# Recurrence feeding an FFN on one core: r transposed raw, exponentials multiplied out of PSUM, row loads of four batches, masks and small products dealt out anew

## The chip, the cores and the metric

One core of a Trainium2 chip. The metric is the time of one execution in microseconds (us). The two kernels compute the same thing in bf16 with fp32 sums, and both are correct. A run is called fast unless it is over 1.5% above the fastest of its kernel; only fast runs are compared.

## The reference, cut

```python
# r, k, v, w: (4 batches, 8 heads, 768 steps, 48);  u: (8, 48)
for t in range(S):                                    # the recurrence (RWKV-6)
    y[t]  = r[t] @ (state + (u * k[t]) outer v[t])
    state = w[t] * state + k[t] outer v[t]
x = y as (3072 tokens, 384)                           # the FFN
out = ((x @ w1) * (x @ w2)) @ w3 @ w_out              # d_ff = 1024
```

The kernel takes the steps in 6 chunks of 128. With cumulative sums c of log w in a chunk, it forms K = k·exp(−c) and R = r·exp(c up to the step before), a masked 128x128 product M of K and R per head, then y = M·v + R·state + dv. Here dv is the diagonal term v·(sum of r·k·u). w3 and w_out are multiplied together once, beforehand.

## The kernel before

The work is cut into 13 units (one or two batches of one chunk) and 8 FFN blocks (up to 512 tokens). A list scheduler in the kernel plans one order of issue from model durations and tuned priority tables; each engine then executes its own operations strictly in that order. The parts that matter, cut:

```python
UNITS = [(0, 0, 1), (0, 1, 1), (0, 2, 2)] + [(c, b, 2) for c in range(1, 6) for b in (0, 2)]
DMA_KR = PE_DIAG = set(range(9, 13))      # K, R and r*k of these units are transposed by DMA
SP_LOADS = {("w", 0)}                     # every other row load is issued by GpSimd (k, r, v change type)
NI = 5                                    # row buffers of two batches: win, kin, rin; six for v
# --- unit t (cut) ---
ACT  lw = Ln(w)
PE   CS = LT^T @ lw                       # running sums in PSUM, by step
ACT  iw = Exp(-lw);  NEt = Exp(-CS);  Et = Exp(CS)          # all to SBUF
DVE  rw = r * iw
DVE  KR[k] = k * NEt;  KR[r] = rw * Et                      # both inputs in SBUF
DVE  rk = r * k;  ruk = rk * u;  dg = reduce_sum(ruk)
POOL dv = v * dg
PE   transposes of KR (k and r) -> PSUM;  ACT KRT = copy    # or two DMA transposes
PE   M = K^T R;  DVE Mbf = M * mask                         # 5 of 24 masks: ACT copy, then POOL select
PE   y = R state + M v;  DVE yb = y + dv;  PE transpose;  ACT xT = copy
PE   kv;  DVE T = kv + S;  POOL Sbf = T * pc, S = T * pc
# --- block n: 8 pairs of a, b matmuls; ACT a copy; DVE abT = a * b; then out = abT @ (w3 w_out) ---
```

## Time and profile before

| kernel before | value |
|---|---|
| median of the first 3 runs | 186.49 us (184.28 to 186.94) |
| profiled run: time, span, mean granted clock | 186.09 us, 184.4 us, 0.986 |
| busy: TensorE, VectorE, ScalarE, GpSimd | 157.5, 131.4, 110.1, 108.0 us |

The busy shares, the stretches and the chain of waits are shown in the prediction. These are 2 us stretches of the kernel before. The columns are the stretch, busy time (with instruction count) of TensorE, its weight loads, VectorE, ScalarE and GpSimd, then the granted clock, the DMA share and GB/s.

```profile
92.00:94.00 2.00, 1.01 (x7) 0.39 (x4) 2.00 (x3) 0.48 (x1) 1.98 (x3) 1.00 2.14 159
94.00:96.00 2.00, 0.00 (x0) 0.00 (x0) 2.00 (x3) 0.00 (x0) 1.83 (x2) 1.00 2.37 162
96.00:98.00 2.00, 1.72 (x27) 1.51 (x28) 1.99 (x4) 0.80 (x1) 0.00 (x0) 0.87 1.24 112
98.00:100.00 2.00, 2.00 (x21) 2.00 (x20) 1.81 (x3) 1.36 (x1) 0.00 (x0) 0.50 0.96 176
100.00:102.00 2.00, 2.00 (x73) 1.67 (x73) 0.58 (x1) 1.72 (x2) 0.04 (x1) 0.78 1.08 370
```

TensorE stands still for 3.27 us, and 1.2 us after it starts again its clock is halved. The Trainium skill says in "TensorE: Matmul & The Clock Gate", section HAM oscillation — how this bites in real kernels, that idle gaps of more than about 3.4 us bring the half-rate clock back. This trace roughly agrees, at 3.27 us.

### The profile page before, as it was taken

How to read it: one execution, taken by the hardware profiler on the slowest of the kernel's cores; microseconds unless marked ns; L12 is line 12 of the kernel's file. 1: busy time of each engine (PE TensorE's matmuls, PEld its weight loads, DVE VectorE, ACT ScalarE, POOL GpSimd, SP SyncE). 2: the span in 40 equal slices, each digit the busy share in tenths (PEclk: the TensorE clock that was granted, in tenths of full speed). 3: DMA queues.
4: the chain of work that ended last, by engine and by line, in shares of the span. 5: the costliest groups of instructions: out<-in, count | busy, mean ns of one | idle time of the engine just before them, and what ended most of it. 6: DMA issues, size and time to landing. Idle time of an engine off the chain costs nothing.

```text
span 184.4 us, 4285 instructions
## 1 busy us (share of the span) xinstructions
PE 157.5 (85%) x1753; PEld 98.8 (54%) x1753; DVE 131.4 (71%) x205; ACT 110.1 (60%) x184; POOL 108.0 (59%) x108
## 2 busy tenths in 40 slices
PE   1242698999989998799929999999999999999991
PEld 0131486787767765346519545665546446545560
DVE  6258858497599986899996996876897286445420
ACT  4261475989988698776817728789732435351321
POOL 7999969976987999989970895132402202000000
PEclk9999999999999999999996999999999999999998
DMA  4999999999999999999999950496604501100332
GB/s 52 193 158 205 195 188 237 155 207 199 165 164 168 187 183 192 176 153 156 142 145 223 112 77 4 88 183 133 117 0 100 146 0 37 52 0 0 128 128 87
DMA packets 95971, 24.13 MB, mean 131 GB/s; under 512 B 88192, under 2 KB 93824, under 8 KB 95952
## 3 DMA queue, kind: packets, MB, share of 16 engines
q0 software_dynamic: 79408, 16.06, 105.1%
q1 hardware_dynamic: 16544, 7.80, 18.4%
q8 instruction: 13, 0.21, 0.5%
q14 instruction: 6, 0.05, 0.1%
HBM read 27.79 MB, written 4.72 MB: 176 GB/s over the span
## 4 chain that ended last, share of the span: by engine, by line
PE 73%; DVE 10%; POOL 5%; issue 4%; DMA 3%; ACT 3%; DVEq 0%; POOLq 0%
PE banks L802 18%; PE banks L807 16%; PE banks L825 14%; PE banks L567 4%; PE banks L676 4%; PE banks L694 3%; DMA kin<-in_k_dram 3%; PE banks L733 3%; PE banks L598 2%; PE banks L753 2%; DVE Mbf L700 2%; PE banks L555 2%; DVE yb L742 2%; DVE KR L630 2%; PE banks L727 2%
## 5 line engine op out<-in xcount | busy, mean ns | idle before, releaser
L814 ACT COPY a_sb<-banks 128x512 f32<-128x512 f32 (+2 forms) x64 | 30.1, 483 | 30.1 <-PE banks L802 23.4
L818 DVE TENSOR_TENSOR abT<-a_sb,banks 128x512 bf16<-128x512 f32 (+2 forms) x64 | 34.1, 550 | 17.4 <-PE banks L807 14.1
L802 PE MATMUL banks<-xT,w_bf 128*128 128x512 bf16 (+2 forms) x192 | 39.3, 335 | 1.4 <-DVE abT L818 1.4
L807 PE MATMUL banks<-xT,w_bf 128*128 128x512 bf16 (+2 forms) x192 | 39.3, 329 | 0.0
L825 PE MATMUL banks<-w,abT 128*128 128x384 bf16 x192 | 33.7, 326 | 0.0
L802 PEld LDWEIGHTS <-w_bf 128*128 128x128 bf16 x192 | 17.4, 102 | 14.9 <-issue 1.9
L825 PEld LDWEIGHTS <-abT 128*128 128x128 bf16 x192 | 18.1, 98 | 11.7
L700 DVE TENSOR_TENSOR Mbf<-banks,mask 128x1024 bf16<-128x1024 f32 x19 | 23.0, 1218 | 1.0 <-PE banks L694 1.0
L807 PEld LDWEIGHTS <-w_bf 128*128 128x128 bf16 x192 | 16.7, 99 | 13.0
L658 POOL TENSOR_TENSOR dv<-vin,dg 128x768 bf16<-128x768 bf16 (+1 forms) x13 | 18.9, 1463 | 7.8 <-issue 2.4
L682 ACT COPY KRT<-banks 128x2048 bf16<-128x2048 bf16 (+1 forms) x9 | 15.1, 1674 | 7.8 <-PE banks L676 7.4
L513 POOL DMA_DIRECT2D vin<-in_v_dram x13 | 14.8, 1140 | 7.8 <-issue 7.8
L676 PE MATMUL banks<-I,KR 128*128 128x128 bf16 x128 | 11.4, 250 | 8.7 <-DVE KR L628 7.4
L780 POOL TENSOR_TENSOR Sbf<-Tst,pc 128x384 bf16<-128x384 f32 (+1 forms) x11 | 9.2, 835 | 13.6 <-PE banks L727 13.5
L742 DVE TENSOR_TENSOR yb<-banks,dv 128x768 bf16<-128x768 f32 (+1 forms) x13 | 11.6, 894 | 5.5 <-PE banks L733 5.2
L513 POOL DMA_DIRECT2D kin<-in_k_dram x13 | 14.4, 1112 | 1.4 <-DVE rk L634 0.6
L833 ACT COPY osb<-banks 128x384 f32<-128x384 f32 x16 | 7.7, 481 | 12.6 <-PE banks L825 12.5
L591 ACT ACTIVATE lw<-win 128x768 bf16<-128x768 f32 (+1 forms) x13 | 10.5, 806 | 7.8 <-DMA win<-in_w_dram 7.8
L676 PEld LDWEIGHTS <-KR 128*128 128x128 bf16 x128 | 9.4, 113 | 9.8 <-DVE KR L628 7.6
L513 POOL DMA_DIRECT2D rin<-in_r_dram x13 | 14.6, 1127 | 0.0
L758 ACT COPY xT<-banks 128x768 bf16<-128x768 bf16 (+1 forms) x13 | 9.8, 755 | 7.8 <-PE banks L753 7.8
L706 POOL TENSOR_SCALAR_AFFINE_SELECT Mbf<-Mbf 128x1024 bf16<-128x1024 bf16 x5 | 6.2, 1231 | 13.9 <-ACT Mbf L703 13.9
(66 smaller groups left out, 249.8 us busy)
## 6 DMA issues: line engine op xcount, KB each, us to landing
out_dram<-osb SPq DMA_DIRECT2D x24, 192.0 KB, 2.0
win<-in_w_dram POOLq DMA_DIRECT2D x11, 384.0 KB, 10.2
kin<-in_k_dram POOLq DMA_DIRECT2D x11, 192.0 KB, 10.4
rin<-in_r_dram POOLq DMA_DIRECT2D x11, 192.0 KB, 9.8
vin<-in_v_dram POOLq DMA_DIRECT2D x11, 192.0 KB, 9.7
w_bf<-in_moe_w_dram POOLq DMA_DIRECT2D x4, 512.0 KB, 10.4
w_bf<-in_moe_w_dram POOLq DMA_DIRECT2D x4, 384.0 KB, 6.3
wo_bf<-in_moe_w_out_dram POOLq DMA_DIRECT2D x1, 768.0 KB, 9.6
```

Of the source, the lines that this page charges most:

```text
L513: op(eng, 60 if eng == "SP" else 700 + 250 * nb, lambda: e.dma_start(dst[:, :nb * H], ap), w=[key], prio=turn_of(f"{src}in_{t}"), dma=nb * ...
L591: op("ACT", act(N), lambda: nc.scalar.activation(LW[:, :, :D], ww, Act.Ln), r=[kw, "table"], w=[f"lw{s}"], prio=pr, name=f"ln_{t}")
L658: op("POOL", pool(N), lambda: nc.gpsimd.tensor_mul(dvs, vv, dgs[:, :, None].to_broadcast([C, bh, D])), r=[f"dg{s}", kv], w=[f"dv{s}"], pri ...
L676: nc.tensor.transpose(o[:, b, q, :], KRs[:, x, h:h + 2, :].rearrange("t h d -> t (h d)"), I128)
L682: nc.scalar.copy(KRTs.rearrange("p x b q t -> p x (b q t)"), o[:, :, :nb * HP * C])
L700: nc.vector.tensor_mul(Mbf[m].rearrange("s j q t -> s (j q t)"), o.rearrange("s j f -> s (j f)"), mask.rearrange("s q t -> s (q t)"))
L742: nc.vector.tensor_add(ybs.rearrange("t b (q e d) -> t e (b q) d", e=2, d=D), o, dvs.rearrange("t (b q e) d -> t e (b q) d", b=nb, e=2))
L802: nc.tensor.matmul(banks[:, g.at(A), :T], lhsT=wt[:, di, fi * P:(fi + 1) * P], rhs=xT[x][:, di, :T], start=(di == 0), stop=(di == DI - 1))
L807: nc.tensor.matmul(banks[:, g.at(Bk), :T], lhsT=wt[:, di, fi * P:(fi + 1) * P], rhs=xT[x][:, di, :T], start=(di == 0), stop=(di == DI - 1))
L814: nc.scalar.copy(a_sb[sa][:, :T], banks[:, g.at(A), :T])
L818: nc.vector.tensor_mul(abT[x][:, fi, :T], a_sb[sa][:, :T], banks[:, g.at(Bk), :T])
L825: nc.tensor.matmul(banks[:, g.at(O), :DM], lhsT=abT[x][:, fi, tt * P:(tt + 1) * P], rhs=w34[:, fi, :], start=(fi == 0), stop=(fi == FI - 1))
```

## The change

Its intent is to take work off the two elementwise engines, at the price of more TensorE work, and to issue fewer and larger row loads:

- r is transposed as loaded. The sums are made a second time, transposed (CT), so exp(CT) multiplies r^T straight out of PSUM. iw, rw and one multiply go.
- exp(−sum) is written back into PSUM, and k is multiplied there.
- From chunk 1 on, one load brings four batches. Buffers hold three chunks.
- Masks, r·k, r·k·u, dv, copies and state products are dealt out anew among VectorE, ScalarE and GpSimd: 13 masks instead of 5 go over ScalarE and GpSimd, and 13 of the r·k and r·k·u products go to GpSimd.
- Only units 11 and 12 keep DMA transposes, which wait for the last row. The first three blocks get their own buffers.
- The tuned tables, and with them the whole order of issue, are new.

```diff
-DMA_KR = set(range(9, 13))
-PE_DIAG = set(range(9, 13))
+DMA_KR = set(range(11, 13))
+DMA_R = set(range(11, 13))
+PE_DIAG = set(range(2, 5))
-SP_LOADS = {("w", 0)}
+SP_LOADS = {("w", 0), ("w", 1)}
 ... (tables RANK, STEP, ENGINE: all numbers new)
     def loads(t):
+        c, b0, nb = UNITS[t]
+        if c and b0:
+            return
+        for src, x in (("w", win), ("k", kin), ("r", rin), ("v", vin)):
+            load(x[c % NI], src, t, b0, B if c else nb)
 ... (unit)
-           nc.scalar.activation(IW, LW[:, :, :D], Act.Exp, scale=-1.0)
-           nc.vector.tensor_mul(RW, rr, IW)
-            nc.scalar.activation(N_..., o[:, :nb, :DM], Act.Exp, scale=-1.0)
+            nc.scalar.activation(o[:, :nb, :DM], o[:, :nb, :DM], Act.Exp, scale=-1.0)
-        nc.vector.tensor_mul(KRs[:, 0, :, :D], kk, N_)
-        nc.vector.tensor_mul(KRs[:, 1, :, :D], RW, E_)
+            nc.vector.tensor_mul(Ks..., kk..., o[:, :nb])               # o is PSUM
+                    nc.tensor.matmul(o[:, b, q, :], lhsT=LW..., rhs=LT)  # CT
+                        nc.tensor.transpose(o[:, b, q, :], rr..., I128)
+                nc.vector.tensor_mul(KRTs[:, 1]..., o[:, :nb * HP, :], ET[:, :, :C])
 ... (buffers of the first blocks; masks, copies and products by ENGINE)
```

## The prediction

> **What bounds the kernel now.** I read the page's busy shares first, then the busy time in stretches of 10 us, then the chain of waits, and last the timeline of VectorE and GpSimd where the chain leaves TensorE.
>
> ```profile
> PE 157.5 (85%) x1753; PEld 98.8 (54%) x1753; DVE 131.4 (71%) x205; ACT 110.1 (60%) x184; POOL 108.0 (59%) x108
> PE 73%; DVE 10%; POOL 5%; issue 4%; DMA 3%; ACT 3%; DVEq 0%; POOLq 0%
> ```
>
> TensorE is the busiest engine and carries 73% of the chain. That says nothing of when, so the stretches (columns: PE, PEld, DVE, ACT, POOL, then granted clock, DMA share, GB/s):
>
> ```profile
> 10.00:20.00 10.00, 3.87 (x48) 2.62 (x45) 6.52 (x11) 3.43 (x7) 9.97 (x12) 1.00 1.91 182
> 70.00:80.00 10.00, 7.81 (x75) 4.17 (x72) 8.81 (x13) 7.36 (x12) 9.38 (x9) 1.00 2.30 183
> 90.00:100.00 10.00, 6.73 (x69) 5.13 (x69) 9.80 (x10) 4.15 (x6) 5.81 (x6) 0.87 2.08 150
> 140.00:150.00 10.00, 10.00 (x75) 5.16 (x70) 5.33 (x8) 4.20 (x7) 1.70 (x2) 1.00 0.45 113
> ```
>
> The reader is to see three regimes: a start in which TensorE is mostly idle and GpSimd full; a middle (to about 105 us) in which rows are still loaded, VectorE is over 8.8 of 10 and TensorE has holes; and an end in which TensorE alone is full. The chain says what the holes wait for (columns: start, us, what):
>
> ```profile
> 9.77 6.00 DMA kin<-in_k_dram
> 15.86 0.67 DVE KR L628
> ...
> 87.66 2.72 DVE KR L630
> ...
> 163.49 0.65 PE banks L802 x3
> 164.14 0.65 PE banks L807 x3
> ```
>
> At the start it is the second unit's k rows, which land at 15.77 us; in the middle one VectorE multiply; at the end matmuls back to back, 0.65/3 = 0.216 us each. The timeline shows that multiply among its neighbours, and GpSimd beside it:
>
> ```profile
> 87.19 0.55 DVE L628 TENSOR_TENSOR KR<-kin,NEt 128x768 bf16<-128x768 bf16 x1
> 87.66 4.36 DVE L630 TENSOR_TENSOR KR<-rw,Et 128x768 bf16<-128x768 bf16 x1
> 88.68 2.92 POOL L658 TENSOR_TENSOR dv<-vin,dg 128x768 bf16<-128x768 bf16 x2
> ```
>
> The same shape took 0.55 us just before and 4.36 us here, with GpSimd busy without a break beside it.
>
> To size the holes I count TensorE's work at the pace that the chain shows when nothing waits: 384 columns 0.1625 us (eight in 1.30), 128 columns 0.056 (six in 0.34), one column 0.0225 (eight in 0.18), the half-height pairs 0.041 (eight in 0.33). Over all 1753 matmuls that is about 146 us. The span is 184.4, the last matmul ends near 180.4, so some 34 us are lost: about 15 up to 30 us, 3 from 30 to 70, about 10 from 70 to 105, 1.5 after that; the few that remain are rounding of paces. The end cannot be shortened except by less TensorE work; the start and the middle can.
>
> **What the Trainium skill says.** "GPSIMD Engine Reference", section Key points: it shares its SBUF interfaces with VectorE and contends with VectorE instructions that have two SBUF inputs. The trace agrees: 4.36 against 0.55 us above, and means of 0.75 to 0.93 us for four of the five such multiplies. "VectorE: DVE Perf Modes", section The perf-mode tier table: a bf16 tensor_tensor runs at 2x from SBUF, at 1x with any PSUM operand. The trace agrees: 550 ns for 768 columns from SBUF, 957 ns for 768 out of PSUM, 1218 for 1024. "TensorE: Matmul & The Clock Gate", section Back-to-back issue gap: N/2.4 + 2.5 ns, with a floor near 25 ns; the paces above agree (0.216, 0.056, 0.0225). "ScalarE: Activation LUTs", section Step-by-step: what each stage is for: writing PSUM is faster than writing SBUF. Nothing in this trace writes PSUM from ScalarE, so I take no gain for it.
>
> **The change part by part** (counts from the two programs as built, durations from the groups by shape).
>
> TensorE. Gone: 96 one-column sums (2.2 us), 128 transposes of k and r (7.2), 24 small dg matmuls (0.6). New: 96 transposed sums of 128 columns (5.4), 160 transposes of k and r, since only units 11 and 12 keep the DMA path (9.0), 18 transposes of r*k for units 2 to 4 (1.0), 18 dg matmuls (0.45). Net +5.8 us, 152 in all. Where TensorE is full this is a loss one for one.
>
> VectorE. Gone: r*iw 9.4, r*E 11.4, k*NE 7.1, eight masks at 1.218 = 9.7, and 6.8 of r*k and 3.4 of r*k*u, which GpSimd takes: 47.8. New: k times the exp in PSUM, 11 x 0.957 + 2 x 0.55 = 11.6; r^T times E^T, 11 x 1.218 + 2 x 0.7 = 14.8; copies of k^T 2.9 and rk^T 1.7; dv 4.0, xT 2.6, state products 2.6, and 2.1 for outputs and dg: 42.3. Net about -5.5, to 126. More to the point, multiplies with both inputs in SBUF fall from 61 to about 23, so GpSimd can hold up far fewer of them.
>
> ScalarE. Gone: iw 10.4, pc 2.1, the double KRT copy 15.1, some xT 3.7 and 1.4 of others; new: E of 1024 columns instead of 768 +2.3, k^T copies 6 x 1.01 = 6.1, eight more mask copies +8.1. Net -16, off the path.
>
> GpSimd. 51 row loads cost 57.7. Now 4 of 16 heads at 1.15, 7 of 8 heads at 0.9 and 20 of 32 heads; eight heads more cost 0.25, so I estimate 1.65 each: 44. Plus r*k 11.9, r*k*u 7.9 and masks 9.8; minus dv 6.3, states 4.2, mask constant 1.2: +4 in sum, but most of the added work comes after the loads are issued.
>
> DMA. The bytes are the same. The landing records of the trace give a pace: k of 16 heads every 1.45 us, w 1.9, a w1 piece 2.0, a w3 piece 2.45, wo 3.8. All rows and weights need about 100 us at any grain; before, the last row lands at 107.6.
>
> The start. The new issue order puts k and r of the second unit sixth and ninth. At the paces above k lands at 12.0 (was 15.77), r at 15.5, v at 16.3, so the first block's matmuls start near 18 us instead of 22.6. Then wo (31), v of unit 2 (33), and v of the four-batch chunk 1 (48) gate again, since a four-batch load lands late for its first half. At 50 us I count 31.5 us of TensorE work done against 26.8 before: 4.7 ahead, of which 2.2 is added work. Net gain 2.5.
>
> The middle. Of the 10 us lost between 70 and 105 I expect 7.5 to go: the held-up multiplies are gone and the GpSimd queue is lighter while loads are issued. Own buffers for the first blocks and the wait of the DMA transposes for the last row remove waits that the trace shows small (transposes among loads took 6.1 us to land, 3.0 alone); I give them nothing extra.
>
> Sum: 184.4 - 2.5 (start, net) + 3.6 (the rest of the added TensorE work) - 7.5 (middle) = 178.0 of span. The profiled run's time was 186.09 for that span, 1.7 more: **179.7 us**, 3.6% under the median of 186.49.
>
> **The rivals.** (a) VectorE stays the bound of the middle. For it: its sum falls only 5.5 us, and the new multiplies run at 1x. Then the middle gives 2 or 3 us, which the added TensorE work eats: about 184. (b) GpSimd becomes the wait: 13 masks instead of 5 go from ScalarE over GpSimd to TensorE, in a strict queue behind loads that wait for buffers. For it: before, such masks waited on ScalarE, not on GpSimd (13.9 us of idle), so nobody has tested that queue. About 185 to 188. (c) The loads of four batches bring rows too late for chunk 2 (v near 69 us), and TensorE idles once more between 50 and 70. Against it: about 17 us of work lie ready there. Costs 2 or 3 us: 182. (d) All holes go, and only the start and the added work remain: 174 to 175.
>
> **Range and chances.** My middle case is 179.7. (a) to (c) pull up, (d) down, hence 174 to 185 for 8 in 10. Faster by over 2% means under 182.8: 0.70, as start and middle must both fail to lose it. Within 2%: 0.21. Slower needs (b): 0.09.
>
> **What would show it.** Right: the first block's matmuls begin near 18 us; TensorE busy above 9 in each stretch from 30 to 105 us; the clock at 1.00 throughout; no VectorE multiply above 2 us; TensorE instruction count near 1801; loads of 32 heads at about 1.65 us on GpSimd; the rT multiply near 1.2 us. Wrong: VectorE over 9.5 with holes in TensorE (a); TensorE idle released by GpSimd's mask (b); idle released by v or w rows between 50 and 75 us (c). If TensorE is dense from 20 us and the time is still above 183, then my paces for the added matmuls are too small.

## The result, and the profile after

The changed kernel is correct. It takes 179.7 us (median of 4 runs, 179.53 to 180.0). The kernel before took 185.7 us (median of 4 in the same rounds, 184.28 to 186.94). The ratio of the fast runs is 0.968, 95% interval 0.960 to 0.976. Every ratio here is the mean time of one kernel's fast runs over that of the kernel before in the same rounds, so it is not quite the ratio of the medians.

These lines of the page after answer to the busy shares and the chain by engine that the prediction shows of before:

```profile
PE 161.6 (91%) x1800; PEld 102.2 (57%) x1800; DVE 129.6 (73%) x204; ACT 98.2 (55%) x157; POOL 109.8 (62%) x97
PEclk9999999999999999999999999999999999999999
PE 75%; DMA 15%; POOL 6%; issue 1%; DVE 1%; ACT 0%; POOLq 0%; DVEq 0%
```

VectorE's share of the chain falls from 10% to 1%, though its busy time falls by only 1.8 us. The clock row has a 9 in each of its 40 slices, but its first part means nothing: the trace's first record of the clock is at 20.2 us, and at 25.8 us in the kernel before, and where there is no record the views print full clock. Up to there the matmuls ran at about half pace. These are nine matmuls of 128 columns in the kernel before (nine such at 31.18 us took 0.68), then nine in the changed kernel:

```profile
22.42 1.12 PE L802 MATMUL banks<-xT,w_bf 128*128 128x128 bf16 x9
```

```profile
20.32 0.68 PE L896 MATMUL banks<-xT,w_bf 128*128 128x128 bf16 x9
```

TensorE was busy for 10.4 us up to that point before and for 10.6 after, so the slow clock cost both about 5 us (an estimate: half of that); in the changed kernel it ended 5.6 us earlier. The prediction has no such term, and no run tests what set the moment. The same stretches as of before:

```profile
10.00:20.00 10.00, 7.57 (x83) 5.64 (x82) 7.32 (x15) 4.59 (x5) 7.93 (x12) 1.00 1.80 189
70.00:80.00 10.00, 10.00 (x92) 4.67 (x91) 9.20 (x14) 6.51 (x11) 9.34 (x7) 1.00 2.50 148
90.00:100.00 10.00, 9.79 (x138) 6.16 (x138) 8.15 (x10) 6.54 (x10) 9.28 (x9) 1.00 1.91 209
140.00:150.00 10.00, 10.00 (x98) 4.47 (x97) 7.79 (x10) 4.26 (x7) 1.09 (x1) 1.00 0.04 16
```

The hole of the middle is gone: TensorE is at 9.79 in the stretch where it was at 6.73, although GpSimd is busier there (9.28 against 5.81) and VectorE still busy. The chain of waits after (start, us, what) has, from 40.7 us to the last output, hardly anything but TensorE (0.6 us of VectorE at 89.6). Up to there it reads:

```profile
8.79 7.34 DMA rin<-in_r_dram
16.21 0.85 POOL rk L673
17.06 8.09 DMA rin<-in_r_dram
25.29 1.63 POOL rk L673
26.92 1.69 POOL win L549
28.61 11.03 DMA kin<-in_k_dram
39.74 0.96 DVE Kt L668
```

The start is now a chain of row loads: r of a unit lands, GpSimd multiplies it, and issues the next loads behind that.

To see where the time came from I count TensorE's work by stretch, each matmul at its median pace per form. This count gives 132.5 us for before and 138.1 after, less than the prediction's 146 and 152, since the half-height matmuls start in pairs a few ns apart, and a median pace miscounts them in both; the difference of 5.6 is what is used. Counted with the prediction's paces the first four rows gain 3.3, 1.5, 6.3 and 0.9 us, so a row is good to about half a microsecond.

| stretch | work before | work after | gained |
|---|---|---|---|
| 0 to 50 us | 24.3 | 27.6 | +3.3 |
| 50 to 70 us | 16.5 | 17.9 | +1.5 |
| 70 to 110 us | 27.7 | 33.5 | +5.8 (1.7 of it the clock) |
| after 110 us | 64.1 in 74.4 us | 59.1 in 67.9 us | +1.5 (lost 8.8 instead of 10.3) |
| more work to do | | | −5.6 |
| sum | | | 6.5 = 184.4 − 177.9 |

### The profile page after: what moved, and what is told of

Read it like the earlier page. It is cut to its first block, busy times and chain, and to the rows that moved or that the text cites. A ratio compares the mean times of both kernels' runs of the same rounds, so it can differ in the third digit from the quotient of the medians.

```text
span 177.9 us, 4339 instructions
## 1 busy us (share of the span) xinstructions
PE 161.6 (91%) x1800; PEld 102.2 (57%) x1800; DVE 129.6 (73%) x204; ACT 98.2 (55%) x157; POOL 109.8 (62%) x97
## 4 chain that ended last, share of the span: by engine, by line
PE 75%; DMA 15%; POOL 6%; issue 1%; DVE 1%; ACT 0%; POOLq 0%; DVEq 0%
PE banks L914 18%; PE banks L896 16%; PE banks L891 16%; DMA rin<-in_r_dram 9%; DMA kin<-in_k_dram 6%; PE banks L605 4%; PE banks L770 4%; PE banks L815 3%; PE banks L650 3%; PE banks L751 2%; PE banks L732 2%; PE banks L842 2%; PE banks L804 2%; PE banks L859 2%; POOL win L549 2%; PE banks L643 1%
## 5 line engine op out<-in xcount | busy, mean ns | idle before, releaser
L891 PEld LDWEIGHTS <-w_bf 128*128 128x128 bf16 x192 | 16.3, 98 | 13.5 <-issue 0.9
L779 ACT CAST Mbf<-banks 128x1024 bf16<-128x1024 f32 x13 | 13.2, 1013 | 5.6 <-PE banks L770 5.5
L776 DVE TENSOR_TENSOR Mbf<-banks,mask 128x1024 bf16<-128x1024 f32 x11 | 13.5, 1223 | 3.7 <-PE banks L770 3.5
L714 POOL TENSOR_TENSOR dv<-vin,dg 128x768 bf16<-128x768 bf16 x8 | 11.8, 1477 | 7.0 <-PE banks L842 6.9
L668 DVE TENSOR_TENSOR Kt<-kin,banks 128x768 bf16<-128x768 bf16 (+1 forms) x13 | 11.4, 887 | 4.6 <-DMA kin<-in_k_dram 4.3
L673 POOL TENSOR_TENSOR rk<-rin,kin 128x768 bf16<-128x768 bf16 (+1 forms) x8 | 12.4, 1547 | 3.6 <-DMA rin<-in_r_dram 3.6
L737 DVE TENSOR_TENSOR KRT<-banks,eT 128x1024 bf16<-128x1024 bf16 (+1 forms) x11 | 12.4, 1123 | 3.0 <-PE banks L732 1.8
L663 ACT ACTIVATE eT<-banks 128x1024 f32<-128x1024 f32 (+1 forms) x13 | 12.4, 958 | 2.9 <-PE banks L650 2.8
L824 DVE TENSOR_TENSOR dv<-banks,dv 128x768 bf16<-128x768 f32 (+1 forms) x13 | 11.6, 891 | 2.7 <-PE banks L815 2.4
L634 ACT ACTIVATE lw<-win 128x768 bf16<-128x768 f32 (+1 forms) x13 | 10.1, 791 | 5.9 <-DMA win<-in_w_dram 5.8
L657 ACT ACTIVATE banks<-banks 128x768 f32<-128x768 f32 (+1 forms) x13 | 9.7, 749 | 5.7 <-PE banks L643 5.5
L605 PE MATMUL banks<-wo_bf,w3T 128*128 128x384 bf16 x64 | 11.7, 326 | 0.0
```

The source lines that it names most:

```text
L605: nc.tensor.matmul(o[:, :DM], lhsT=w3T[fi % 2][:, gi, :], rhs=wo_bf[:, gi, :], start=(gi == 0), stop=(gi == FI - 1))
L663: nc.scalar.activation(ET[:, :, 1:], o[:, :nb * HP, :], Act.Exp)
L673: op("DVE", {"DVE": dve(N, 2), "POOL": 1490}, lambda e: ENG[e].tensor_mul(rks, rr[:, :, :D], kk), r=[*kr, *kk_], w=[f"rk{s}"], prio=pr + 8 ...
L776: nc.vector.tensor_mul(Mbf[m].rearrange("s j q t -> s (j q t)"), o.rearrange("s j f -> s (j f)"), mask.rearrange("s q t -> s (q t)"))
L779: nc.scalar.copy(Mbf[m].rearrange("s j q t -> s j (q t)"), banks[:, g.at(MM):g.at(MM) + 2, :])
L891: nc.tensor.matmul(banks[:, g.at(A), :T], lhsT=wt[:, di, fi * P:(fi + 1) * P], rhs=xT[x][:, di, :T], start=(di == 0), stop=(di == DI - 1))
```

## The experiments

The order of issue depends on every operation, and with its tuned tables the scheduler found no plan at all for any of the dozen variants with one part changed. So in all runs the order was planned from the unaltered kernel, and the part was exchanged when the operations were emitted in that order. That isolates a part; it doesn't show what a new plan could have made of it. The edits are shown shortened. Labels with a are variants of the changed kernel (179.7 us), labels with b of the kernel before (185 us in the same rounds). Differences to the changed kernel are taken between medians of different rounds; taken between the ratios they come out up to 0.9 us larger.

### The multiplies that GpSimd holds up

**b_exp_psum**: the exp in PSUM alone, in the kernel before.

```diff
-  nc.scalar.activation(E_..., o, Act.Exp)
+  nc.scalar.activation(o if t in IN_PSUM else E_..., o, Act.Exp)      # ten units
-  nc.vector.tensor_mul(KRs[:, 1], RW, E_)
+  nc.vector.tensor_mul(KRs[:, 1], RW, banks[CS])                      # where t in IN_PSUM
```

In five units the exp of minus the sum is also moved ahead of this one, which now overwrites the sum that both read.

> The kernel before, with one part of the change alone: for ten of thirteen units the exp of the sum is written back into PSUM and the r multiply reads it there (about 0.96 us, 1x), instead of from SBUF (0.55 us when free, 4.36 us when held up by GpSimd). The issue order is otherwise that of before. Theory H (what the middle of before loses are VectorE multiplies with both inputs in SBUF that wait for GpSimd): the 4.36 us multiply disappears, TensorE work between 70 and 110 us grows by 2 to 5 us, time 1.5 to 4 us shorter. Rival B (only the sum of VectorE's busy time counts): ten multiplies longer by 0.4 us each, so 1 to 4 us slower.

Measured: 184.58 us, ratio 0.997 (0.994 to 0.999). The 4.36 us multiply is gone, and nearly nothing is won. Two groups of VectorE in this run (counts, then busy us and mean ns):

```profile
L610 DVE TENSOR_TENSOR rw<-rin,iw 128x768 bf16<-128x768 bf16 x11 | 9.8, 894 | 0.0
L635 DVE TENSOR_TENSOR KR<-rw,banks 128x768 bf16<-128x768 bf16 x9 | 8.5, 948 | 1.0 <-ACT banks L620 0.9
```

The multiply out of PSUM takes its steady 948 ns, but r·iw, still with both inputs in SBUF, now takes 894 ns on average (748 before). The hold-up moved to the next multiply of that kind: one r·iw took 2.27 us at 90.8. TensorE still waits 2.1 us for a y sum at 95 us. Theory H had TensorE's work between 70 and 110 us right in the profiles (3.2 us more, 1.7 of it the clock), but not the time: the runs with a mean clock of at least 0.997 have a median of 184.58 us here (10 runs) and 184.53 in the kernel before (18).

**a_ne_sb**: the same part undone in the changed kernel.

```diff
-  nc.scalar.activation(o, o, Act.Exp, scale=-1.0)            # in PSUM
+  nc.scalar.activation(NEs, o, Act.Exp, scale=-1.0)          # to SBUF
-  nc.vector.tensor_mul(Ks, kk, o)
+  nc.vector.tensor_mul(Ks, kk, NEs)
```

> The changed kernel with one part undone, in the same issue order: the exp of minus the sum goes to SBUF again and the k multiply reads both inputs from SBUF. Theory H: some of these multiplies are held up by GpSimd and take over 1.2 us in the stretch from 30 to 105 us, and the time rises by 1 to 3 us. Rival B: VectorE's sum falls by up to 4 us (0.55 instead of 0.95 us each), and the time is the same or up to 1 us shorter.

Measured: 179.11 us, ratio 0.968 (0.962 to 0.973), the same as the changed kernel's. Its k multiply, and that of the changed kernel:

```profile
L668 DVE TENSOR_TENSOR Kt<-kin,NEs 128x768 bf16<-128x768 bf16 x11 | 8.1, 743 | 2.2 <-DMA kin<-in_k_dram 2.1
```

```profile
L668 DVE TENSOR_TENSOR Kt<-kin,banks 128x768 bf16<-128x768 bf16 x11 | 10.3, 947 | 1.8 <-DMA kin<-in_k_dram 1.6
```

From SBUF it is sometimes held up (743 ns on average instead of 550), and still shorter than out of PSUM. In this order this part of the change is worth nothing.

**b_no_iw**: r·iw and its exp taken away from the kernel before. Its output is wrong, which doesn't matter for the time.

```diff
-  nc.scalar.activation(IW, LW, Act.Exp, scale=-1.0)
-  nc.vector.tensor_mul(RW, rr, IW)
-  nc.vector.tensor_mul(KRs[:, 1], RW, E_)
+  nc.vector.tensor_mul(KRs[:, 1], rr, E_)
```

> The kernel before with r*iw and its exp taken out and nothing put in their place (so a wrong result on purpose); issue order kept. It takes about 9.4 us off VectorE and 10.4 off ScalarE, spread over all units. Theory V (the sum of VectorE's work in the stretch from 70 to 105 us makes TensorE's hole there): the hole shrinks, the time falls by 2 to 4 us. Rival P (TensorE's own fixed order of work and the data it stands behind make the hole, so a lighter VectorE only waits more): time within 1 us of before.

Measured: 185.94 us, ratio 1.000 (0.996 to 1.005). Some 9.8 us off VectorE and 9.2 off ScalarE (121.6 and 100.9 busy) bought nothing. In its timeline (start, us, engine, line, what), first VectorE, then GpSimd:

```profile
86.42 4.15 DVE L634 TENSOR_TENSOR rk<-rin,kin 128x768 bf16<-128x768 bf16 x1
90.49 1.21 DVE L700 TENSOR_TENSOR Mbf<-banks,mask 128x1024 bf16<-128x1024 f32 x1
91.63 0.94 DVE L742 TENSOR_TENSOR yb<-banks,dv 128x768 bf16<-128x768 f32 x1
97.84 0.56 DVE L634 TENSOR_TENSOR rk<-rin,kin 128x768 bf16<-128x768 bf16 x1 [2.25 <-DMA rkT<-rk]
...
87.01 2.92 POOL L658 TENSOR_TENSOR dv<-vin,dg 128x768 bf16<-128x768 bf16 x2
```

Here is TensorE's second wait in this run, and the y sum of the kernel before:

```profile
99.32 0.51 PE L753 MATMUL banks<-I,yb 128*128 128x128 bf16 x6 [2.21 <-DVE yb L742]
```

```profile
95.28 0.94 DVE L742 TENSOR_TENSOR yb<-banks,dv 128x768 bf16<-128x768 f32 x1
```

The hold-up is still there, now on r·k (4.15 us). The y sum (yb) needs dv from GpSimd, but dv does not come last: it ends at 89.93, and yb begins at 91.63, behind the held-up r·k and a mask in VectorE's fixed order. In the kernel before dv ended at 91.60 and yb began at 95.28. TensorE's wait for this yb fell from 3.27 to 1.31 us. In its place came a wait of 2.21 us for the next yb: in front of it r·k stood for 2.25 us, waiting for the DMA transpose of the r·k before it (rkT). Together that is 3.5 us of holes, and the same 1.7 us of lost clock. So time taken off VectorE went into other waits. The run does not show what the kernel would do without any hold-up. One reserve: every run of this variant had a mean clock of 0.990 or less, so up to about 1 us of gain may hide in the clock.

**a_rk_dve**: all r·k and r·k·u back on VectorE in the changed kernel.

```diff
-  o.fn(o.eng)
+  o.fn("DVE" if o.kind in ("rk", "ruk") else o.eng)
```

> The changed kernel with r*k and r*k*u back on VectorE for all units (13 multiplies moved off GpSimd, 1.64 us each there), in the same issue order. Theory H: VectorE gets 13 more multiplies with both inputs in SBUF, at least 7 us of work, more where they are held up; TensorE loses 2 to 5 us between 40 and 105 us and the time rises as much. Rival (GpSimd's multiplies stand in front of the row loads and delay them): loads are issued sooner, VectorE has the room, time the same or 1 to 3 us shorter.

Measured: 180.39 us, ratio 0.976 (0.969 to 0.983), some 0.7 us longer; the lower end of what the hold-up theory expected was 2. GpSimd falls to 90.9 busy without a gain: this share of GpSimd's work was not on the path.

### The start

**b_order**: the first loads of the kernel before in the order of the changed one.

```diff
+  seq = ["win_1", "w1_0", "kin_0", ..., "kin_1", "vin_0", "win_2", "rin_1", "vin_1", "w2_0", "kin_2", ...]
+  for i, x in zip(places, seq): order[i] = ops[x]
-  e = nc.sync if eng == "SP" else nc.gpsimd
+  e = nc.sync if src == "w" and t < 2 else nc.gpsimd
```

> The kernel before with the issue order of the first loads taken from the changed kernel (w of the second unit on the other queue, k, r and v of the second unit and the first weight pieces earlier), nothing else. Theory S (start and middle add up, as in the prediction): k of the second unit lands near 13 us, the first block's matmuls begin near 18 to 19 us, and the time falls by 2 to 3.5 us. Rival (the lead of the start is waited away in the middle, where VectorE and the rows set the pace): the same start, but time within 1 us of before.

Measured: 185.39 us, ratio 1.002 (0.999 to 1.005). Both expectations were off at the start: k of the second unit landed at 9.84 us, even earlier, yet the first block began only at 20.95 us (22.42 before):

```profile
20.95 1.12 PE L802 MATMUL banks<-xT,w_bf 128*128 128x128 bf16 x9
```

Between them lies the unit's own chain of multiplies, transposes, masks and the y sum, each in its engine's fixed order. By 50 us this variant had done 23.3 us of TensorE work, before 24.3. The line shows one more cause: 1.12 us for nine such matmuls is the slow pace, and this trace has its first record of the clock only at 29.0 us, with TensorE busy for 13.5 us up to there (10.4 in the kernel before, to 25.8). By the estimate above that is 6.7 us lost instead of 5.2, more than the missing 1.0. In this profile, then, the slow clock alone is enough to undo what the earlier start gained. The new load order alone is worth nothing.

### Masks, grain and GpSimd's queue

**b_mask**: eight more masks off VectorE in the kernel before.

```diff
+MOVED = {(4, 0), (5, 0), (6, 1), (7, 0), (8, 1), (9, 0), (10, 0), (10, 1)}
-  op("DVE", dve(1024), msk, ...)
+  op("DVE", dve(1024), (lambda: (mcp(), maff())) if (t, b) in MOVED else msk, ...)
```

> The kernel before with eight more masks taken from VectorE to ScalarE and GpSimd (units 4 to 10, the division of the changed kernel), order kept. VectorE loses 8 times 1.22, about 9.7 us; ScalarE gets about 8.1, GpSimd about 9.6. Theory V: the time falls by 1.5 to 4 us. Rival: ScalarE is at 8 to 9 of 10 and GpSimd over 9 of 10 between 50 and 90 us in this kernel, so they take the place of VectorE as the wait, and it is the same or up to 3 us slower. That would mean that the masks can move only together with the work that the change takes off ScalarE.

Measured: 189.2 us, ratio 1.022 (1.017 to 1.026). It went the rival's way:

```profile
90.00:100.00 10.00, 8.03 (x144) 5.68 (x142) 5.66 (x7) 8.57 (x11) 9.97 (x10) 1.00 2.50 183
```

```profile
103.85 0.82 PE L755 MATMUL banks<-I,yb 128*128 128x128 bf16 x6 [4.85 <-DVE yb L744]
```

GpSimd is full to 100 us, VectorE is busy for only 5.66 of the last 10, and TensorE's wait for the y sum grows to 4.85 us. The clock is then at half from 100.7 to 107.5 us, which is 3.4 us lost where the kernel before lost 1.7; all four runs have a mean clock of 0.977 to 0.986. So in the profile nearly half of the cost is clock, lost from within the longer hole on.

**a_mask_dve**: the 13 masks back on VectorE in the changed kernel.

```diff
-  lambda e, f=msk, f2=mcp: (f2 if e == "ACT" else f)()      # and POOL select after
+  lambda e, f=msk: f()
```

> The changed kernel with all masks on VectorE: 13 of them go back from ScalarE and GpSimd, about 15.8 us more on VectorE, 13 less on ScalarE, 14 less on GpSimd; order kept. Theory V: VectorE, over 9 of 10 in 70 to 90 us already, becomes the bound of the middle; time longer by 3 to 8 us. Rival P: within 1 us.

Measured: 184.61 us, ratio 0.9965, so 4.9 us longer. VectorE has 140.7 us to do and is the wait in many small places, for instance here:

```profile
120.00:130.00 10.00, 9.00 (x114) 5.36 (x113) 9.88 (x13) 3.21 (x4) 1.30 (x1) 1.00 0.44 110
```

The same move that costs 4 us in the old kernel carries 4 to 5 in the new one: the ten of its 20 runs with a mean clock of at least 0.997 have a median of 184.13 us, 4.4 longer, so about 0.5 of the 4.9 is clock.

**a_two**: the four-batch loads split in two in the changed kernel.

```diff
-  lambda: e.dma_start(dst[:, b0*H:(b0+nb)*H, :D], ap)
+  lambda: [e.dma_start(dst[:, (b0+x)*H:(b0+x+min(nb, 2))*H, :D], ap[:, x*H:(x+min(nb, 2))*H]) for x in range(0, nb, 2)]
```

> The changed kernel with each load of four batches issued as two of two, one after the other in the same place: the same bytes and order in a finer grain. GpSimd pays about 2 times 1.15 instead of 1.7 us for 20 of them, 12 us more in sum. As in the prediction, the grain costs nothing at the transfers: time the same or up to 2 us longer by GpSimd's load. Rival (c) of the prediction (rows of four batches arrive late for their first half): the first half lands over 1 us sooner, and the time falls by 1 us or more.

Measured: 182.84 us, ratio 0.990 (0.986 to 0.993), so 3.1 us longer, more than the prediction's side allowed and opposite to rival (c). Chain by engine, a stretch, and a wait of TensorE:

```profile
PE 50%; POOL 33%; DVE 5%; issue 4%; DMA 4%; ACT 1%; POOLq 0%; DVEq 0%
```

```profile
80.00:90.00 10.00, 8.19 (x98) 4.72 (x95) 9.59 (x12) 5.69 (x10) 10.00 (x9) 1.00 1.26 82
```

```profile
85.59 0.57 PE L815 MATMUL banks<-vin,Mbf 128*128 128x48 bf16 x16 [1.75 <-POOL Mbf L782]
```

GpSimd now holds 33% of the chain instead of 6, is at 10.00 of 10, and TensorE waits for its mask. So the coarser grain is what makes room on GpSimd for the masks. It is rival (b) of the prediction, brought about.

**b_w_sp**: GpSimd freed in the kernel before by giving all loads of w to SyncE.

```diff
-  e = nc.sync if eng == "SP" else nc.gpsimd
+  e = nc.sync if src == "w" else nc.gpsimd
```

> The kernel before with all loads of w (which need no change of type) issued by SyncE instead of GpSimd; order otherwise kept. It takes 12 issues of about 1.16 us, 13.9 us, off GpSimd, the same amount that the four-batch loads take off (13.7), and leaves VectorE, ScalarE and TensorE alone. Theory G, formed after the first eight runs (in the middle GpSimd's queue sets the pace: loads, the dv multiply behind them, the y sum behind that): the hole at 90 to 100 us shrinks and the time falls by 2 to 4 us. Theory V (VectorE's sum) and rival P (TensorE's order): within 1 us. A risk to the reading: SyncE's queue also carries the stores and transposes, which may wait behind a load of w.

Measured: 200.07 us, ratio 1.082. The run doesn't test the middle, since the start went wrong: SyncE had issued seven loads of w by 18 us, ahead of any need, and the other rows came late. GpSimd's own wait says it:

```profile
40.86 2.26 POOL L658 TENSOR_TENSOR dv<-vin,dg 128x768 bf16<-128x768 bf16 x2 [14.39 <-DMA vin<-in_v_dram]
```

One v load took 25.7 us to land where it had taken 10.1. The Trainium skill says in "DMA: Bandwidth & Descriptors", section SWDGE vs HWDGE vs iDMA, that both kinds of queue feed the same engines, which take turns between them; this trace is in line with it.

**b_four**: the four-batch loads alone in the kernel before.

```diff
-  rin, kin, vin, win: 5 or 6 buffers of two batches
+  rin, kin, vin, win: 3 buffers of four batches
-  lambda: e.dma_start(dst[:, :nb * H], ap)
+  (load of all four batches at the first unit's place) if b0 == 0 else (nothing)     # chunks 1 to 5
```

> The kernel before with one part of the change alone: from the second chunk on each row load brings four batches (32 heads) instead of two, 20 loads of about 1.7 us in place of 40 of 1.15, so 12 to 13 us less of GpSimd; buffers for three chunks; the bytes, the other operations and their order are kept. It is the converse of the run that split these loads in the changed kernel and cost 3.1 us, and it has no foreign queue in it as the run with SyncE had. Theory G (GpSimd's queue sets the pace of the middle): the y sums come earlier, the hole at 90 to 100 us shrinks, time 2 to 4 us shorter. Rival V or P (VectorE's sum, or TensorE's order): within 1 us. Rival (c) (first halves land late): 1 to 3 us longer.

Measured: 192.56 us, ratio 1.042 (1.031 to 1.052). GpSimd falls by 12.3 us to 95.7 busy, and the kernel gets slower. The chain, and then TensorE, at 35 to 46 us:

```profile
34.62 10.18 DMA kin<-in_k_dram
44.80 0.02 issue
44.82 0.56 DVE rk L638
```

```profile
45.63 0.49 PE L811 MATMUL banks<-xT,w_bf 128*128 128x128 bf16 x6 [4.48 <-DVE abT L822]
```

In the old order VectorE's r·k of chunk 1 stands ahead of an FFN product (abT). Its k row, now part of a larger load, lands at 44.8 us instead of 39.3, and TensorE's FFN work waits behind it for 4.5 us. After the hole the clock is at half for 3.4 us. By 50 us the variant has 18.5 us of TensorE work done, before 24.3. That is most of the 7 us. The hole near 100 us stays too (2.8 us): the lighter GpSimd alone didn't close it.

### The other terms

**a_dbl_late**: added TensorE work, measured by itself, in the changed kernel.

```diff
+TWICE = {7, 8, 9, 10}
-  nc.tensor.matmul(o[:, b, q, :], lhsT=LW..., rhs=LT)        # likewise both transposes
+  for _ in range(2 if t in TWICE else 1): nc.tensor.matmul(o[:, b, q, :], lhsT=LW..., rhs=LT)
```

> The changed kernel with the 24 matmuls per unit of the transposed sums and of the transposes of r and k issued twice for units 7 to 10: 96 more of 128 columns at 0.056 us, 5.4 us of TensorE work, the same result. If added TensorE work is lost one for one from the middle on, as the prediction has it: 4.5 to 5.5 us longer. Rival (it lies beside waits for GpSimd and VectorE): under 2 us longer.

Measured: 185.35 us (20 runs), 5.6 us longer for 5.4 us of work. TensorE's work from about 85 us on is lost one for one.

**a_undo2**: own block buffers and the late DMA transposes undone together.

```diff
-  xT[slot[blk]], abT[slot[n]]
+  xT[blk % 2], abT[n % 2]
+  put("dtr_11", ahead_of="trr_9"); put("dtr_12", ahead_of="trr_10")
```

> The changed kernel with its two small parts undone together: the first blocks share the two block buffers again, and the two DMA transposes of r stand where the transposes of units 9 and 10 are, among the last row loads, instead of after the last row. The prediction gives these parts nothing: time within 1 us of the changed kernel. Rival (they are needed: the second block waits for the first one's buffer, transposes among loads delay the rows): 1.5 us or more longer.

Measured: 180.09 us, ratio 0.972 (0.964 to 0.979), but with a wrong result, which was not intended. The planned order writes products of the third block (abT) before the output matmuls of the first block have read theirs, so with shared buffers the data were overwritten instead of a wait being added. The run therefore says nothing of what the buffers are worth, only that this order cannot do without them. The early transposes changed no data and cost at most 0.4 us.

## Why the prediction was right or wrong

The time was right: 179.7 predicted and measured. Its sum was right within 0.1 us (6.4 of span predicted, 6.5 measured), but partly by errors that cancel, and the pair of profiles is not typical: the profiled run of the kernel before (186.09 us) lay 1 us above the median of its 99 later runs (185.13), and the medians of the same rounds differ by 6.0 us. Of the signs, TensorE was above 9 in each stretch from 30 to 105 us (the lowest 9.43) and the r^T multiply took 1.22 us; the clock was full where it is recorded.

- **TensorE +5.8**: right. 5.6 by the count, 1800 instructions (1801 expected), and a_dbl_late shows such work to be lost one for one in the later stages.
- **The start, 4.7 us of work ahead at 50 us**: mis-sized, 3.3 measured. The first block began at 19.85 us, not near 18, as k of the second unit landed at 13.1 instead of 12.0. The pace was also misread: up to 25.8 us the old kernel's matmuls ran at half of it, so part of the "about 15 us lost up to 30" was slow clock and not waiting. The reason given (the new load order) is not enough by itself: b_order gained nothing.
- **The middle, 7.5 us**: 5.8 us measured between 70 and 110 us, plus 1.5 between 50 and 70, which the prediction gave nothing. Of the 5.8 us, 1.7 is clock that the hole had cost, and the prediction had no term for it. It also gave nothing after 110 us, where 1.5 was won (0.9 by the prediction's paces).
- **"The held-up multiplies are gone"**: this step failed. They are not all gone: two multiplies took 3.23 us beside GpSimd's dv in the changed kernel, one of them 2.77, against the sign "none above 2 us". Where they stood they cost TensorE little:

```profile
86.46 3.23 DVE L673 TENSOR_TENSOR rk<-rin,kin 128x768 bf16<-128x768 bf16 x2
...
87.78 1.49 POOL L714 TENSOR_TENSOR dv<-vin,dg 128x768 bf16<-128x768 bf16 x1
```

  And their removal isn't what pays: the part alone brought 0.3%, and undoing it cost nothing (b_exp_psum, a_ne_sb). In the old kernel the hold-up passes to the next multiply of its kind (2.27 us on r·iw in b_exp_psum, 4.15 on r·k in b_no_iw), and a shorter wait at one y sum was followed by a new one at the next. No run took all of them out, so what they cost the old kernel in all stays open.
- **"The GpSimd queue is lighter while loads are issued"**: supported in the changed kernel, where splitting the loads again costs 3.1 us. A 32-head load holds GpSimd for about 1.7 us, where 1.65 was estimated.
- **VectorE −5.5**: mis-sized, −1.8 measured. What counted was where its work went: the masks, 4.9 us by a_mask_dve. The prediction only had them as a rival's risk (b). ScalarE fell by 11.9 us, not 16, and GpSimd rose by 1.8, not 4.
- **Rivals**: (a) and (b) did not come to matter (the nearest is 80 to 90 us, with VectorE at 9.97 and TensorE at 9.43), and a_mask_dve and a_two show how near each was: 13 masks more on one engine, or 12 us of issues on the other. (c) was not seen in the changed kernel. In the old order it did come (b_four).
- **Transposes and own buffers, nothing extra**: the transposes' place makes no difference; the buffers are untested.

What is shown: in the new order the move of the masks (4.9 us) and the coarser loads (3.1 us) both carry, and the exp in PSUM, the r·k products on GpSimd (0.7 us) and the transposes' place carry little or nothing. In the old order none of the parts tried pays alone, and masks or grain alone cost 4 to 7 us. By their traces, moved masks need room on GpSimd, and coarse loads need an order that doesn't put a late row ahead of FFN work. What stays open is how much of the gain is the new order itself, with its raw transposes of r, and whether the old operations could be planned as well. No run here had a new plan.

No variant clearly beats the changed kernel: a_ne_sb has the lowest median, 179.11 us, but the same ratio to the kernel before.

## What to carry to other kernels

When a chain of waits names an instruction that another engine holds up, taking that one away need not end the hold-up: here the next of its kind took it over. Compare the end of each input with the start of the instruction that waits for it, to see which really came last. Parts of a change that is planned as a whole don't add up: a move pays only where the receiving engine has room and the order of issue fits, so test each part both alone in the old kernel and undone in the new one. A hole in TensorE costs its length and often some clock; count both, and check the pace of like matmuls where the clock column has no record.

## What the Trainium skill lacked or had wrong

- "SBUF — State Buffer", SBUF: two separate sides, does not say that one VectorE instruction can be held over several of GpSimd in a row. Here a 0.55 us multiply took 4.36 us: it began 1.0 us before the first of GpSimd's two multiplies and ended 0.4 us after the second.
- "ScalarE: Activation LUTs", Step-by-step: writing PSUM is called faster, without a size. The exp of 768 columns took 798 ns to PSUM in the changed kernel and 808 to SBUF in a_ne_sb; in b_exp_psum it took 822 to PSUM and 814 or 821 to SBUF. No run here shows a gain above about 1%, and the kernel gained nothing (ratio 0.968 with and without).
- "TensorE: Matmul & The Clock Gate", HAM oscillation: the gap that brings the slow clock is given as over about 3.4 us. Here the length of one hole did not decide it: spells of slow clock (3.41 us, in b_mask 6.83) followed holes of 3.27, 3.28 and 4.85 us (before, b_order, b_mask), none followed one of 3.25 (b_w_sp), and one came at 100.6 us in b_no_iw, with no hole above 2.21 between 30 us and there. Of 99 runs of the same kernel 61 showed a lowered mean clock, which is 1.1 us in the medians.
- "DMA: Bandwidth & Descriptors" has no figure for how long an issue holds GpSimd by shape. With 128 rows of 48 elements per head it was 0.9 us for 8 heads, 1.15 for 16 and 1.7 for 32, and on this kernel's path that grain was worth 3.1 us.
